# Folding two sections of w_mod on chip, keeping the softmax only transposed, and issuing zero fills from ScalarE in a fused forward and backward block

## The chip, the cores and the metric

One core of one Trainium2 chip runs one program, a single launch with all inputs and outputs in HBM. The metric is device time in microseconds of one execution; beside it stands one execution with the hardware profiler on. The engines are TensorE (PE), VectorE (DVE), ScalarE (ACT), GpSimd (POOL) and SyncE (SP). PE, DVE and ACT compute; in this kernel POOL does nothing but issue transfers after its first microseconds, and SP nothing else at all. 16 DMA engines move the data, whichever engine issued the transfer.

## The reference

One token (D = 1024) goes through an adaLN block: attention over a window of 4096 cached keys (32 query heads, 4 KV heads), then a gated FFN with F = 3584. The outputs are the block's output and the gradients of all its eleven inputs, all bf16.

```python
mod = (silu(c) @ w_mod).reshape(1, 6, 1, -1)          # w_mod [1024, 6144]
sa, ca, ga, sb, cb, gb = (mod[:, i] for i in range(6))
h = layernorm(x) * (1 + ca) + sa
q = h @ wq;  p = softmax(q k^T * Dh**-0.5);  o = p v   # last 4096 of 65536 rows of the caches
x = x + ga * (o @ wo)
h = layernorm(x) * (1 + cb) + sb
x = x + gb * ((sigmoid(h @ w_gate) * (h @ w_up)) @ w_down)
out, vjp = jax.vjp(f, x, k_cache, v_cache, wq, wo, w_gate, w_up, w_down, c, w_mod)
return (out, *vjp(grad_out))
```

The gradients of the two caches have the caches' own shape, [4, 65536, 128]. Of these, 61440 rows of each head lie outside the window and are zero: the kernel writes them as 120 zero fills of 1 MiB each. The gradient of a weight is an outer product of a column and a row, as large as the weight. The gradient that reaches c needs w_mod times the gradient of mod.

## The kernel before

All big data lies in one SBUF tile, `arena`, cut into regions by hand: A (64 KiB of each partition), B and C (32 each), F (40), E (8). The order of every engine is the order of the code (a manual schedule), and each engine issues its transfers in that order.

**Front.** SP loads w_mod (8 tiles of 1.5 MiB, L233), wq (8 of 1 MiB, L237), K and V (L282), wo (L298) and the first w_down blocks. PE multiplies each tile as it lands: `mod_ps` (L257), `q_ps` (L287), transposes of K and V (L318), scores, softmax into a tile of its own, `P_bf`, [128 rows, 4096], its transpose `pT` (L352 to L365), `o_col` (L371), then the product with wo (L417).

**FFN, 7 blocks of 512 columns, L445 to L503.** A block has 1 MiB each of w_down, w_up, w_gate (`wd`, `wu`, `wg`), in five slots of 8 KiB in region F; slot number is `3n`, `3n+1`, `3n+2` modulo 5. So `wg` of block n+1 takes the slot of `wd` of block n once that has been stored, `wd` of n+2 that of `wu` of n, and `wu` of n+2 that of `wg` of n. In a block: PE `gu` (L451), ACT two sigmoids (L455, L456), DVE `dhh` (L458 to L470), PE broadcasts and ACT casts to `du_b`, `dg_b` (L483), DVE overwrites `wd` with its gradient (L485) and POOL stores it (L486); then DVE reduces each of the 8 tiles of `wu` and ACT overwrites it with its gradient (L491, L492), POOL stores it (L493), and the same for `wg` (L498 to L500). POOL also loads `wg` and `wu`; SP loads `wd`. Weights are overwritten in place by their gradients, so a store must land before the next load into that slot.

**Back.** Broadcast of the gradients (L518, L551), wo's part in 8 pieces (DVE L560, ACT L561, store L562; a landed store lets SP load a tile of wq again into that place, L565, tiles 1 to 7, as tile 0 has stayed in region E), the gradient of the scores `dS` (L587, which reads `P_bf`), `dq`, then a loop over 8 tiles (L634 to L644): wq's gradient (L635, L636, stored L637), K's and V's gradients (`grad_kv`, L615 to L629, PE and ACT, stored L628) and, every second turn, a section `sec` (L540): columns 2048 to 6143 of a row tile of w_mod, loaded again by SP (L538), reduced and overwritten by DVE, stored by POOL (L543). At the end, columns 0 to 2047 of w_mod, loaded again by SP as 8 tiles of 512 KiB (L547), are reduced by DVE (L666), and ACT makes their gradient (L667), stored by POOL (L668).

**Zero fills** (`zero`, L124) are put between this work by counts. Before: 42 from POOL in the front, paced by PE, DVE and the counts `Z_MOD` to `Z_LN`; 42 from SP in the FFN, two at each of three places of a block, each with a dependence on the block's work (`Z_FFN`, L489, L494, L503); 36 from POOL in the back.

The transfers of SP and ACT together go round eight completion flags (DMAHW0 to DMAHW7 in the program), those of POOL round another eight (DMASW0 to DMASW7): a transfer waits for the landing of the one that had its flag before it.

Of the kernel before, what the change touches and what calls it, by code (L numbers as in the profile page):

```python
# [10 lines left out]
P = 128  # L11
FP32 = mybir.dt.float32
# [24 lines left out]

Z_MOD, Z_Q, Z_KV, Z_SM, Z_O, Z_WO, Z_LN = 1, 1, 1, 2, 2, 1, 2
Z_FFN = (2, 2, 2)
Z_T0 = 3  # L40
Z_DWO = [1, 1, 1, 1, 1, 1, 1, 6]
Z_SEC = [1, 1, 1, 1, 1, 1, 1, 1]
Z_DWQ = [1, 1, 1, 1, 1, 1, 1, 1]
Z_DKV = [0, 0, 1, 0, 1, 0, 1, 0]


@with_exitstack
def kernel(
# [34 lines left out]

    arena = pool.tile([P, 176 * KIB], BF16, name="arena")

# [3 lines left out]

    A_OFF, B_OFF, C_OFF, F_OFF, E_OFF = 0, 64, 96, 128, 168  # L90

# [77 lines left out]
    def col_to_row_out(col_f, dram_out_row, name):  # L169
        rp = ptp.tile([8, P], FP32, name="rp_" + name, tag="tp")  # L170
        nc.tensor.transpose(rp[:, :], col_f, ident_f[:, :])
        rowb = vt([8, P], name + "_orow", BF16)
        cp(rowb, rp[:, :])
        nc.sync.dma_start(out=dram_out_row.rearrange("o (j p) -> (o j) p", p=P), in_=rowb)
# [60 lines left out]
    wq_t = [ar(E_OFF, 8)] + [ar(A_OFF + 8 * (j - 1), 8) for j in range(1, KD)]  # L235
    for j in range(KD):
        nc.sync.dma_start(out=wq_t[j], in_=wq_view[:, j, :])  # L237

    zero(4)

# [11 lines left out]
    ln1, rstd1 = layernorm_col(x0_col, "ln1")  # L252

    mod_ps = new_acc("mod_ps")
    for j in range(KD):
        for k in range(KM):
            mm = nc.tensor.matmul(mod_ps[:, k:k + 1], lhsT=wm_t[j][:, k * P:(k + 1) * P],  # L257
                                  rhs=cs_bf[:, j:j + 1], start=(j == 0 and k == 0), stop=(j == KD - 1),
                                  skip_group_check=True)
        zero(Z_MOD, mm)  # L260
    mod_col = vt([P, KM], "mod_col")
# [23 lines left out]
    for j in range(KD):  # L285
        for h in range(HQ):
            mm = nc.tensor.matmul(q_ps[:, h:h + 1], lhsT=wq_t[j][:, h * P:(h + 1) * P],  # L287
                                  rhs=h1_bf[:, j:j + 1], start=(j == 0 and h == 0), stop=(j == KD - 1),
                                  skip_group_check=True)
        zero(Z_Q, mm)  # L290
    q_col2 = vt([P, 2 * HQ], "q_col2", BF16)
# [19 lines left out]

    def transpose_kv(src, engs):
        for i in range(16):
            tb, g = divmod(i, G)
            tp = new_tp("tp_kv")
            for t8 in range(8):
                t_ = tb * 8 + t8
                nc.tensor.transpose(tp[:, t8 * P:(t8 + 1) * P], src[:, g, t_ * DH:(t_ + 1) * DH], ident_bf[:, :])  # L318
            o = x_T[:, g, tb * 1024:(tb + 1) * 1024]
            if engs[i] == "A":  # L320
                last = nc.scalar.copy(out=o, in_=tp[:, :])  # L321
            else:
                last = cp(o, tp[:, :])
            if i % 4 == 3:
                zero(Z_KV, last)

    transpose_kv(k_nat, "AV" * 8)
    Q_hd = make_hd(q_col2, "Q_hd")

    P_bf = vt([P, W], "P_bf", BF16)  # L330
    mx8 = vt([P, 8], "mx8")
# [13 lines left out]
    nc.scalar.activation(out=P_bf, in_=P_bf, func=ACT.Exp, bias=nbias[:, 0:1], scale=SCALE, accum_out=ssum)  # L345
    transpose_kv(v_nat, "VVVVVV" + "AV" * 5)
# [3 lines left out]
    zero(Z_SM, last)  # L350

    def transpose_rows(src, name, engs="AVAV"):  # L352
        dst = pool.tile([P, KT, G, HG], BF16, name=name, tag="pTdsT")
        for tb in range(4):
            tp = new_tp("tp_" + name)
            for t8 in range(8):
                t_ = tb * 8 + t8
                nc.tensor.transpose(tp[:, t8 * P:(t8 + 1) * P], src[:, t_ * P:(t_ + 1) * P], ident_bf[:, :])
# [56 lines left out]
    for h in range(HQ):  # L415
        for k in range(KD):
            mm = nc.tensor.matmul(attn_ps[:, k:k + 1], lhsT=wo_t[h // 4][:, h % 4, k * P:(k + 1) * P],  # L417
                                  rhs=o_bf[:, h:h + 1], start=(h == 0 and k == 0), stop=(h == HQ - 1),
                                  skip_group_check=True)
        if h % 4 == 3:  # L420
            zero(Z_WO, mm)
    zero(Z_LN, mm)
# [22 lines left out]
    for n in range(NB):  # L445
# [110 lines left out]
    for q4 in range(8):  # L556
# [24 lines left out]
    for ch in range(8):  # L581
        ps = new_ps("dp_ps")
        for g in range(G):
# [49 lines left out]
    dwq_view = out_4.rearrange("(j p) n -> p j n", p=P)  # L633
    for j in range(KD):  # L634
# [3 lines left out]
        zero(Z_DWQ[j])  # L638
        grad_kv(gkv[8 * j:8 * j + 8], Z_DKV[j])
        if j % 2 == 1:  # L640
            sec(2 + j // 2, Z_SEC[2 + j // 2])
            if j == 1:
                s2_load(6)
                s2_load(7)  # L644

# [66 lines left out]
```

## Time and profile before

| what | value |
|---|---|
| median of 3 runs | 674.62 us (672.17 to 674.93) |
| the profiled execution | 675.23 us |
| its span, first to last instruction | 673.5 us |
| bytes moved in the span | 265.74 MB |
| busy share of the span | DVE 46%, ACT 31%, PE 22%, POOL 14% |

The profiled execution's own time is 1.7 us longer than its span, and 0.6 us longer than the median. A page of the profile gives each engine's busy time, the busy share and rate of the DMA engines in 40 slices of the span, the chain of waits that ended last, groups of equal instructions with what they waited for, and the issues of transfers with the time from issue to landing. `DMA share` in a table of windows is the mean busy share of the 16 DMA engines; 1.0 is all of them.

### The profile page before, as it was taken

To read this page: it belongs to the slowest core of one execution; us is meant where nothing else is said; L and a number is where in the kernel's file an instruction comes from. 1 tells how busy PE (TensorE), PEld (TensorE's weight loads), DVE (VectorE), ACT (ScalarE), POOL (GpSimd) and SP (SyncE) were. 2 spreads that over 40 slices of the span, in tenths; PEclk is the share of its full clock that TensorE was granted. 3 is DMA by queue.
4 is the path that set the end of the run, shared out by engine and by line. 5 is a ranking of instruction groups with operands and counts; after the bars stand their busy time and mean duration, and the time that the engine had idled before them with its cause. 6 is when DMAs were issued, how large, how long until landed. Compare 5 with 4: busy or idle time off the path is not lost.

```text
span 673.5 us, 6855 instructions
## 1 busy us (share of the span) xinstructions
PE 147.2 (22%) x2648; PEld 124.6 (19%) x2648; DVE 307.2 (46%) x604; ACT 209.0 (31%) x304; POOL 96.2 (14%) x161
## 2 busy tenths in 40 slices
PE   2212214661114111111110101304720002333100
PEld 2212213561113101111110001202620001223100
DVE  2000002630008491819180907899842999100790
ACT  1000002730006270707070705796520002334181
POOL 2000100022010101010101010221111111121120
PEclk9999999985555555555555555555755555555555
DMA  8999999999998999999999998999999999999996
GB/s 338 426 428 425 427 425 427 419 419 408 394 423 369 345 377 381 378 373 375 371 380 350 349 415 324 366 422 399 412 416 410 424 425 426 421 423 417 415 407 254
DMA packets 44815, 265.74 MB, mean 395 GB/s; under 512 B 4208, under 2 KB 4208, under 8 KB 19568
## 3 DMA queue, kind: packets, MB, share of 16 engines
q0 software_dynamic: 26640, 156.25, 57.2%
q1 hardware_dynamic: 18096, 109.06, 40.8%
q8 instruction: 20, 0.33, 0.2%
q14 instruction: 11, 0.09, 0.0%
q10 hardware_dynamic: 48, 0.01, 0.0%
HBM read 79.70 MB, written 185.60 MB: 394 GB/s over the span
## 4 chain that ended last, share of the span: by engine, by line
DMA 44%; DVE 8%; issue 5%; ACT 3%; PE 2%; POOL 0%; POOLq 0%; ACTq 0%; DVEq 0%
DMA out_dram<-arena 28%; DMA out_dram<-zeros 9%; DMA arena<-in_B_w_gate_dram 7%; DVE arena L160 4%; DVE junk L160 2%; ACT arena L164 2%; DVE arena L156 1%; PE gu_ps L451 1%; ACT arena L626 1%; ACT arena L624 0%; DVE dug L143 0%; PE ps_kv L620 0%; PE bc_ps L217 0%; ACT dg_b L483 0%; POOL out_dram L500 0%
## 5 line engine op out<-in xcount | busy, mean ns | idle before, releaser
L160 DVE CUSTOM_DVE_ANT_0 arena<-arena 128x4096 bf16<-128x4096 bf16 (+1 forms) x24 | 88.4, 3707 | 22.0 <-DMA arena<-in_w_mod_dram 22.0
L128 POOL DMA_DIRECT2D out_dram<-zeros x78 | 42.4, 544 | 239.8 <-PE mod_ps L257 44.9
L451 PE MATMUL gu_ps<-h_bf,arena 128*128 128x1 bf16 x448 | 16.7, 172 | 156.8 <-DMA arena<-in_B_w_gate_dram 90.4
L321 ACT COPY arena<-tp_kv 128x1024 bf16<-128x1024 bf16 x13 | 13.1, 1010 | 106.2 <-PE tp_kv L318 106.2
L451 PEld LDWEIGHTS <-arena 128*128 128x128 bf16 x448 | 16.1, 118 | 158.5 <-issue 158.5
L143 DVE TENSOR_TENSOR hh<-sg,gu_ps 128x4 f32<-128x4 f32 x7 | 1.1, 159 | 92.4 <-ACT om L456 92.4
L624 ACT CAST arena<-ps_kv 128x512 bf16<-128x512 f32 x32 | 16.1, 697 | 76.1 <-DMA out_dram<-arena 76.1
L160 DVE CUSTOM_DVE_ANT_0 arena<-arena,b1k 128x1024 bf16<-128x1024 bf16 x32 | 36.7, 1218 | 0.0
L160 DVE CUSTOM_DVE_ANT_0 arena<-arena,du_b 128x512 bf16<-128x512 bf16 x56 | 34.9, 689 | 2.0 <-ACT du_b L483 2.0
L164 ACT ACTIVATE arena<-dg_b,h 128x512 bf16<-128x512 bf16 x56 | 35.0, 712 | 0.0
L164 ACT ACTIVATE arena<-du_b,h 128x512 bf16<-128x512 bf16 x56 | 34.9, 712 | 0.0
L160 DVE CUSTOM_DVE_ANT_0 arena<-arena,dg_b 128x512 bf16<-128x512 bf16 x56 | 34.8, 688 | 0.0
L160 DVE CUSTOM_DVE_ANT_0 junk<-arena,b1k 128x1024 bf16<-128x1024 bf16 x28 | 34.2, 1222 | 0.5
L164 ACT ACTIVATE arena<-b1k,o_col 128x1024 bf16<-128x1024 bf16 x32 | 33.4, 1173 | 0.0
L455 ACT ACTIVATE sg<-gu_ps 128x4 f32<-128x4 f32 x7 | 1.2, 173 | 101.1 <-PE gu_ps L451 101.1
L620 PE MATMUL ps_kv<-DO_hd,P_bf 8*128 8x128 bf16 x128 | 15.2, 278 | 76.8 <-ACT arena L624 76.1
L152 DVE COPY arena<-tp_kv 128x1024 bf16<-128x1024 bf16 x19 | 13.0, 691 | 30.3 <-PE tp_kv L318 30.2
L620 PEld LDWEIGHTS <-P_bf 8*128 8x128 bf16 x128 | 11.8, 122 | 80.1 <-issue 78.8
L318 PE MATMUL tp_kv<-ident_bf,arena 128*128 128x128 bf16 x256 | 21.3, 246 | 23.7 <-DMA arena<-in_A_k_cache_dram 15.4
L626 ACT ACTIVATE arena<-ps_kv 128x512 bf16<-128x512 f32 x32 | 16.1, 628 | 31.5 <-DMA out_dram<-arena 31.5
L318 PEld LDWEIGHTS <-arena 128*128 128x128 bf16 x256 | 18.4, 111 | 26.5 <-DMA arena<-in_A_k_cache_dram 16.3
L620 PE MATMUL ps_kv<-Q_hd,arena 8*128 8x128 bf16 x128 | 16.1, 296 | 31.5 <-ACT arena L626 31.5
(179 smaller groups left out, 364.9 us busy)
## 6 DMA issues: line engine op xcount, KB each, us to landing
out_dram<-zeros POOLq DMA_DIRECT2D x78, 1024.0 KB, 23.2
out_dram<-arena POOLq DMA_DIRECT2D x53, 1024.0 KB, 18.5
out_dram<-zeros SPq DMA_DIRECT2D x42, 1024.0 KB, 10.4
arena<-in_A_wq_dram SPq DMA_DIRECT2D x15, 1024.0 KB, 25.5
arena<-in_w_mod_dram SPq DMA_DIRECT2D x8, 1536.0 KB, 27.1
arena<-in_A_wo_dram SPq DMA_DIRECT2D x8, 1024.0 KB, 40.1
arena<-in_w_mod_dram SPq DMA_DIRECT2D x8, 1024.0 KB, 18.2
arena<-in_B_w_up_dram POOLq DMA_DIRECT2D x7, 1024.0 KB, 13.8
```

Of the source, the lines that this page charges most:

```text
L128: ins = (q or nc.gpsimd).dma_start(out=zleft.pop(0), in_=zeros[:, :])
L152: return nc.vector.tensor_copy(out=out, in_=a)
L156: return nc.vector.tensor_scalar(out=out, in0=a, scalar1=s1, scalar2=None, op0=op0)
L160: return nc.vector.tensor_tensor_reduce(out=out, in0=w, in1=b, scale=1.0, scalar=0.0, op0=ALU.mult, op1=ALU.add, accum_out=acc)
L164: return nc.scalar.activation(out=out, in_=b, func=ACT.Copy, scale=col)
L318: nc.tensor.transpose(tp[:, t8 * P:(t8 + 1) * P], src[:, g, t_ * DH:(t_ + 1) * DH], ident_bf[:, :])
L321: last = nc.scalar.copy(out=o, in_=tp[:, :])
L451: nc.tensor.matmul(gu[:, half * 4 + jj:half * 4 + jj + 1], lhsT=w[:, j, jj::4], rhs=h2_bf[:, j:j + 1], start=(j == 0), stop=(j == KD - 1))
L455: nc.scalar.activation(out=sg, in_=gu[:, 0:4], func=ACT.Sigmoid)
L620: nc.tensor.matmul(ps[:, t4 * DH:(t4 + 1) * DH], lhsT=rows[32 * g:32 * g + HG, t_ * P:(t_ + 1) * P], rhs=hd[32 * g:32 * g + HG, :], start= ...
L624: nc.scalar.copy(out=o, in_=ps[:, :])
L626: nc.scalar.activation(out=o, in_=ps[:, :], func=ACT.Copy, scale=float(scale))
```

## The change

1. **w_mod's first two sections.** The gradient to c needs, of columns 0 to 2047, `dsa` times w0 plus `dca` times w1, and `dca` is `dsa` times `ln1`. So w0 + ln1·w1 is formed on chip while w_mod lies there for the forward product (`make_w01`, 2 DVE operations on [128, 1024] for each row tile), and kept in a new region G of 16 KiB. The 8 loads of 512 KiB (L547) are gone, the last DVE reduction is over 1024 columns and not 2048, and the gradient tiles are made by ACT and DVE in turn.
2. **Softmax.** `P_bf` now lies in region F until it has been transposed; `pT` stays. In the back 128 PE transposes and 4 ACT copies rebuild `P_bf` from `pT`, ahead of wo's part.
3. **FFN.** ACT issues the zero fills, at five places of a block and without dependences of their own; SP stores `wd`'s gradient, which POOL did; SP's next load of `wd` stands last in the block.
4. **wq** tile 0 is no longer kept in E: all 8 tiles are loaded again, tile 0 last, and the loop of the back takes them in the order 1 to 7, 0. The loads of `sec` tiles 1 to 6 come after them, that of tile 7 in the loop.
5. **Counts of zero fills**: 29 in the front, 59 in the FFN, 32 in the back, by lists.

```diff
-Z_FFN = (2, 2, 2)
+Z_FFN = [0, 2, 0, 3, 5, 2, 0, 0, 2, 6, 1, 1, 0, 1, 5, 0, 0, 3, 1, 4, 2, 2, 2, 2, 0, 0, 3, 7, 1, 0, 0, 0, 0, 4, 0]
-Z_T0 = 3
+Z_T0 = 6
...
+    w01 = ar(G_OFF, 16).rearrange("p (j n) -> p j n", j=KD)
+    w01_tmp = ar(F_OFF + 32, 4).bitcast(FP32)
+    def make_w01(j):
+        mulv(w01_tmp, wm_t[j][:, D:2 * D], b1k)
+        addv(w01[:, j, :], w01_tmp, wm_t[j][:, 0:D])
...
-    P_bf = vt([P, W], "P_bf", BF16)
+    P_bf = ar(F_OFF + 32, 8)
...
+        zero(Z_FFN[5 * n], None, nc.scalar)
         for jj in range(4):
             last = outer_dve(wd[:, jj, :], hh[:, jj:jj + 1], b1k)
-        nc.gpsimd.dma_start(out=wd_dram(out_8, n), in_=wd_t[n])
+        nc.sync.dma_start(out=wd_dram(out_8, n), in_=wd_t[n])
         if n + 1 < NB:
             load_wg(n + 1)
-        zero(Z_FFN[0], last, nc.sync)
         for j in range(KD):
             ttr(wu[:, j, :], wu[:, j, :], du_b, dh2acc[:, n * 16 + j:n * 16 + j + 1])
             last = outer_act(wu[:, j, :], h2[:, j:j + 1], du_b)
+            if j % 4 == 3:
+                zero(Z_FFN[5 * n + 1 + j // 4], None, nc.scalar)
         nc.gpsimd.dma_start(out=dwu_view[:, :, n * FB:(n + 1) * FB], in_=wu)
...
+    for tb in range(4):
+        tp = new_tp("tp_P")
+        for t8 in range(8):
+            for g in range(G):
+                k = (tb * 8 + t8) * HQ + HG * g
+                nc.tensor.transpose(tp[32 * g:32 * g + 32, t8 * P:(t8 + 1) * P], pT[:, k:k + 32], ident_bf[:, :],
+                                    tile_position=(0, 32 * g))
+        nc.scalar.copy(out=P_bf[:, tb * 1024:(tb + 1) * 1024], in_=tp[:, :])
...
-        ttr(s2_t[j], s2_t[j], dmod_b2, dcs[:, KD + j:KD + j + 1])
-        outer_act(s2_t[j], cs_col[:, j:j + 1], dmod_b2)
+        ttr(w01[:, j, :], w01[:, j, :], dmod_b2[:, 0:D], dcs[:, KD + j:KD + j + 1])
+        if j % 2 == 0:
+            outer_act(s2_t[j], cs_col[:, j:j + 1], dmod_b2)
+        else:
+            outer_dve(s2_t[j], cs_col[:, j:j + 1], dmod_b2)
```

On SP's queue, in the first two blocks of the FFN, stands before (with the flags that each row waits for):

```order
L400 DMA arena<-in_B_w_down_dram 128x4096 [waits DMASW7_49,DMAHW1_49,DMASW0_49,PE_49]
L128 DMA out_dram<-zeros 128x4096 [waits DMAHW2_49,Activation_49]
L128 DMA out_dram<-zeros 128x4096 [waits DMAHW3_49]
L128 DMA out_dram<-zeros 128x4096 [waits DMAHW4_49,DVE_49]
L128 DMA out_dram<-zeros 128x4096 [waits DMAHW5_49]
L128 DMA out_dram<-zeros 128x4096 [waits DMAHW6_49,Activation_49]
L128 DMA out_dram<-zeros 128x4096 [waits DMAHW7_49]
```

and now, at the same place:

```order
L512 DMA out_dram<-arena 128x4096 [waits DMAHW5_49,DMAHW3_49,DVE_49]
L426 DMA arena<-in_B_w_down_dram 128x4096 [waits DMASW1_49,DMASW7_49,PE_49,Activation_49]
L512 DMA out_dram<-arena 128x4096 [waits DMAHW4_49,DMAHW2_49,DVE_49]
L426 DMA arena<-in_B_w_down_dram 128x4096 [waits DMASW5_49,DMAHW5_49,PE_49,Activation_49]
L512 DMA out_dram<-arena 128x4096 [waits DMAHW6_49,DMAHW3_49,DVE_49]
```

The zero fills with their waits for DVE and ACT have left SP; in their place stands the store of `wd`'s gradient, which waits for DVE.

On ScalarE, from the end of the first block to the second block's first gradient tiles, stands before:

```order
L164 ACTIVATE arena<-dg_b,h_1712 128x512 x8
L455 ACTIVATE sg_1976<-gu_ps 128x4
L456 ACTIVATE om_1977<-gu_ps 128x4
L483 CAST du_b<-bc_ps 128x4x128
L483 CAST dg_b<-bc_ps 128x4x128
L164 ACTIVATE arena<-du_b,h_1712 128x512 x8
```

and now:

```order
L172 ACTIVATE arena<-dg_b,h_1730 128x512 [waits DVE_49] x4
L136 DMA out_dram<-zeros 128x4096 [waits DMAHW4_49]
L136 DMA out_dram<-zeros 128x4096 [waits DMAHW5_49]
L136 DMA out_dram<-zeros 128x4096 [waits DMAHW6_49]
L136 DMA out_dram<-zeros 128x4096 [waits DMAHW7_49]
L136 DMA out_dram<-zeros 128x4096 [waits DMAHW0_49]
L480 ACTIVATE sg_1997<-gu_ps 128x4 [waits PE_49]
L481 ACTIVATE om_1998<-gu_ps 128x4
L508 CAST du_b<-bc_ps 128x4x128 [waits PE_49,Activation_49]
L508 CAST dg_b<-bc_ps 128x4x128 [waits PE_49,Activation_49]
L136 DMA out_dram<-zeros 128x4096 [waits DMAHW1_49]
L136 DMA out_dram<-zeros 128x4096 [waits DMAHW3_49]
```

Five zero fills now stand on ScalarE ahead of the next block's sigmoid, and two behind its casts, each with a wait for a flag of an earlier transfer.

On ScalarE at the start of the back stands before:

```order
L222 CAST b1k<-bc_ps 128x512
L222 CAST arena<-bc_ps 128x512 x8
L164 ACTIVATE arena<-b1k,o_col 128x1024 x32
L362 COPY dsT<-tp_dsT 128x256 x4
L222 CAST arena<-bc_ps 128x512 x8
```

and now:

```order
L230 CAST b1k<-bc_ps 128x512
L230 CAST arena<-bc_ps 128x512 x8
L584 COPY arena<-tp_P 128x1024 x4
L172 ACTIVATE arena<-b1k,o_col 128x1024 x32
L389 COPY pT<-tp_dsT 128x256 x4
L230 CAST arena<-bc_ps 128x512 x8
```

The four copies of the rebuilt softmax stand ahead of the 32 operations that make wo's gradient.

More of the change, by code (lines that the diff above doesn't have):

```diff
@@ L35 @@
 KIB = 512
-Z_MOD, Z_Q, Z_KV, Z_SM, Z_O, Z_WO, Z_LN = 1, 1, 1, 2, 2, 1, 2
-Z_FFN = (2, 2, 2)
-Z_T0 = 3
[L41 to L44, printed above, removed]
+Z_INIT = 5
+Z_MOD = [0, 1, 0, 1, 0, 0, 0, 0]
+Z_Q = [2, 0, 0, 1, 0, 1, 0, 2]
+Z_K = [0, 1, 0, 1]
+Z_V = [0, 3, 0, 0]
+Z_SM = 4
+Z_O = 1
+Z_WO = [0, 0, 1, 1, 4, 0, 0, 0]
+Z_LN = 0
+Z_FFN = [0, 2, 0, 3, 5, 2, 0, 0, 2, 6, 1, 1, 0, 1, 5, 0, 0, 3, 1, 4, 2, 2, 2, 2, 0, 0, 3, 7, 1, 0, 0, 0, 0, 4, 0]
+Z_T0 = 6
+Z_DWO = [1, 0, 1, 1, 1, 2, 0, 5]
+Z_SEC = [1, 2, 0, 0, 0, 2, 2, 7]
+Z_DWQ = [0, 2, 0, 2, 0, 0, 2, 3]
+Z_DKV = [0, 1, 1, 0, 0, 1, 1, 0]
 @with_exitstack
@@ L82 @@
     ptp = ctx.enter_context(tc.tile_pool(name="ptp", bufs=2, space=bass.MemoryType.PSUM))
-    arena = pool.tile([P, 176 * KIB], BF16, name="arena")
+    arena = pool.tile([P, 184 * KIB], BF16, name="arena")
     def ar(off, size):
         return arena[:, int(off * KIB):int((off + size) * KIB)]
-    A_OFF, B_OFF, C_OFF, F_OFF, E_OFF = 0, 64, 96, 128, 168
+    A_OFF, B_OFF, C_OFF, F_OFF, G_OFF = 0, 64, 96, 128, 168
     def vt(shape, name, dt=FP32):
@@ L171, in col_to_row_out @@
         nc.tensor.transpose(rp[:, :], col_f, ident_f[:, :])
-        rowb = vt([8, P], name + "_orow", BF16)
+        rowb = pool.tile([8, P], BF16, name=name + "_orow", tag="orow")
         cp(rowb, rp[:, :])
@@ L234 @@
         wm_t.append(t)
-    wq_t = [ar(E_OFF, 8)] + [ar(A_OFF + 8 * (j - 1), 8) for j in range(1, KD)]
+    wq_t = [ar(A_OFF + 8 * ((j + 7) % 8), 8) for j in range(KD)]
     for j in range(KD):
         nc.sync.dma_start(out=wq_t[j], in_=wq_view[:, j, :])
-    zero(4)
+    zero(Z_INIT)
     tp0 = ptp.tile([P, 24], BF16, name="tp_rows", tag="tp")
@@ L252 @@
     ln1, rstd1 = layernorm_col(x0_col, "ln1")
+    ln1_bf = vt([P, KD], "ln1_bf", BF16)
+    cp(ln1_bf, ln1)
+    b1k = vt([P, D], "b1k", BF16)
+    bcast(ln1_bf, KD, b1k, "A")
+    w01 = ar(G_OFF, 16).rearrange("p (j n) -> p j n", j=KD)
[3 more added lines that the diff above has]
+        addv(w01[:, j, :], w01_tmp, wm_t[j][:, 0:D])
     mod_ps = new_acc("mod_ps")
@@ L259 @@
                                   skip_group_check=True)
-        zero(Z_MOD, mm)
+        if j < KD - 1:
+            make_w01(j)
+        zero(Z_MOD[j], mm)
     mod_col = vt([P, KM], "mod_col")
@@ L289 @@
                                   skip_group_check=True)
-        zero(Z_Q, mm)
+        zero(Z_Q[j], mm)
     q_col2 = vt([P, 2 * HQ], "q_col2", BF16)
@@ L324, in transpose_kv @@
             if i % 4 == 3:
-                zero(Z_KV, last)
-    transpose_kv(k_nat, "AV" * 8)
+                zero(nz[i // 4], last)
+    transpose_kv(k_nat, "AV" * 8, Z_K)
     Q_hd = make_hd(q_col2, "Q_hd")
-    P_bf = vt([P, W], "P_bf", BF16)
+    P_bf = ar(F_OFF + 32, 8)
     mx8 = vt([P, 8], "mx8")
@@ L350 @@
     zero(Z_SM, last)
+    pT = vt([P, KT * HQ + 32], "pT", BF16)
+    nc.vector.memset(pT[:, KT * HQ:], 0.0)
     def transpose_rows(src, name, engs="AVAV"):
-        dst = pool.tile([P, KT, G, HG], BF16, name=name, tag="pTdsT")
+        dst = pT[:, 0:KT * HQ].rearrange("p (t g h) -> p t g h", t=KT, g=G)
         for tb in range(4):
@@ L420 @@
         if h % 4 == 3:
-            zero(Z_WO, mm)
+            zero(Z_WO[h // 4], mm)
     zero(Z_LN, mm)
@@ L499 @@
             last = outer_act(wg[:, j, :], h2[:, j:j + 1], dg_b)
+            if j % 4 == 3:
+                zero(Z_FFN[5 * n + 3 + j // 4], None, nc.scalar)
         nc.gpsimd.dma_start(out=dwg_view[:, :, n * FB:(n + 1) * FB], in_=wg)
@@ L502 @@
             load_wu(n + 2)
-        zero(Z_FFN[2], last, nc.sync)
+        if n + 2 < NB:
+            load_wd(n + 2)
     ffn = vt([P, KD], "ffn")
@@ L531 @@
     dcs = vt([P, 2 * KD], "dcs")
-    sec_off = [F_OFF + 24, F_OFF + 32, A_OFF + 56, C_OFF + 16, C_OFF + 24, B_OFF, B_OFF + 8, B_OFF + 16]
+    sec_off = [F_OFF + 32, C_OFF + 16, C_OFF + 24, B_OFF, B_OFF + 8, B_OFF + 16, B_OFF + 24, F_OFF + 24]
     sec_t = [ar(o, 8) for o in sec_off]
-    s2_off = [B_OFF + 24, B_OFF + 28, F_OFF + 24, F_OFF + 28, F_OFF + 32, F_OFF + 36, A_OFF + 56, A_OFF + 60]
-    s2_t = [ar(o, 4) for o in s2_off]
+    s2_t = [ar(A_OFF + 4 * j, 4) for j in range(KD)]
+    P_bf = ar(F_OFF + 24, 8)
     def sec_load(j):
@@ L563 @@
         zero(Z_DWO[q4])
-        if q4 < 7:
-            nc.sync.dma_start(out=wq_t[q4 + 1], in_=wq_view[:, q4 + 1, :])
-    sec_load(2)
+        j = (q4 + 1) % 8
+        nc.sync.dma_start(out=wq_t[j], in_=wq_view[:, j, :])
     do_col2 = vt([P, 2 * HQ], "do_col2", BF16)
@@ L594 @@
     dq_ps, mm = av_like(k_nat, dsT, "dq")
-    sec_load(5)
-    sec_load(6)
-    sec_load(7)
+    for k in range(3, 7):
+        sec_load(k)
     dq_bf = vt([P, HQ], "dq_bf", BF16)
@@ L633 @@
     dwq_view = out_4.rearrange("(j p) n -> p j n", p=P)
-    for j in range(KD):
+    for i in range(KD):
+        j = (i + 1) % 8
         ttr(wq_t[j], wq_t[j], dq_b, dh1[:, j:j + 1])
@@ L637 @@
         nc.gpsimd.dma_start(out=dwq_view[:, j, :], in_=wq_t[j])
[L638 to L644, printed above, removed]
+        zero(Z_DWQ[i])
+        grad_kv(gkv[8 * i:8 * i + 8], Z_DKV[i])
+        if i == 4:
+            sec_load(7)
+        if i % 2 == 1:
+            sec(2 + i // 2, Z_SEC[2 + i // 2])
     dln1 = vt([P, KD], "dln1")
```

21 lines of the change are left out of this document (6 added, 15 removed).

## Prediction

> **What bounds the kernel now.** I read the page first, then a table of windows by stage.
>
> ```profile
> span 673.5 us, 6855 instructions
> ...
> DMA  8999999999998999999999998999999999999996
> GB/s 338 426 428 425 427 425 427 419 419 408 394 423 369 345 377 381 378 373 375 371 380 350 349 415 324 366 422 399 412 416 410 424 425 426 421 423 417 415 407 254
> DMA packets 44815, 265.74 MB, mean 395 GB/s; under 512 B 4208, under 2 KB 4208, under 8 KB 19568
> ```
>
> ```profile
> 10.00:205.00 195.00, 60.71 (x1382) 53.71 (x1383) 25.92 (x67) 26.34 (x32) 23.59 (x41) 0.84 1.02 420
> 205.00:424.00 219.00, 30.58 (x715) 27.71 (x712) 122.21 (x357) 86.65 (x141) 25.81 (x32) 0.50 0.95 368
> 424.00:640.00 216.00, 54.79 (x552) 42.53 (x552) 138.12 (x152) 77.20 (x121) 37.96 (x67) 0.52 1.01 414
> 640.00:660.00 20.00, 0.38 (x1) 0.08 (x1) 18.10 (x23) 16.01 (x8) 4.94 (x11) 0.50 1.01 405
> 660.00:673.50 13.50, 0.00 (x0) 0.00 (x0) 0.00 (x0) 0.00 (x0) 0.49 (x1) 0.50 0.54 217
> ```
>
> The last two columns are the DMA share and GB/s. The DMA engines bound the kernel: in the front (10 to 205 us) and the back (424 to 660) they are all busy, at 405 to 420 GB/s, while no compute engine is busy for more than two thirds of a long stage. The FFN (205 to 424) is the exception: 368 GB/s at a share of 0.95. I went on into one of its blocks by windows, then by the chain of waits (start, length, what).
>
> ```profile
> 265.40:272.70 7.30, 3.23 (x72) 2.83 (x72) 5.42 (x15) 1.71 (x4) 0.89 (x2) 0.50 0.90 281
> 272.70:290.10 17.40, 1.20 (x32) 1.14 (x32) 12.13 (x36) 10.60 (x17) 0.56 (x1) 0.50 1.00 417
> 290.10:299.40 9.30, 0.05 (x2) 0.08 (x3) 0.00 (x0) 0.00 (x0) 2.65 (x3) 0.50 1.00 381
> 272.70:299.40 26.70, 1.24 (x34) 1.22 (x35) 12.13 (x36) 10.60 (x17) 3.21 (x4) 0.50 1.00 404
> ```
>
> ```profile
> 272.69 16.89 DMA out_dram<-arena
> ...
> 290.15 9.07 DMA arena<-in_B_w_gate_dram
> ...
> 306.60 16.46 DMA out_dram<-arena
> ```
>
> A block takes 33.9 us (272.69 to 306.60), and 26.0 of them are two transfers one behind the other: the store of w_down's gradient, then the load of w_gate into the freed slot. While SP's zero fills flow, the rate is 417. When they have run out and only w_gate's load and two gradient stores are left it is 381, and during the block's compute 281. The zero fills come in bursts tied to the block's work, and so leave these holes.
>
> **The change, part by part.** First the bytes, by the issues of transfers (count, size, median us to landing):
>
> ```profile
> out_dram<-zeros POOLq DMA_DIRECT2D x78, 1024.0 KB, 23.2
> out_dram<-zeros SPq DMA_DIRECT2D x42, 1024.0 KB, 10.4
> arena<-in_A_wq_dram SPq DMA_DIRECT2D x15, 1024.0 KB, 25.5
> arena<-in_B_w_up_dram POOLq DMA_DIRECT2D x7, 1024.0 KB, 13.8
> arena<-in_B_w_gate_dram POOLq DMA_DIRECT2D x7, 1024.0 KB, 9.6
> arena<-in_B_w_down_dram SPq DMA_DIRECT2D x7, 1024.0 KB, 6.6
> arena<-in_w_mod_dram SPq DMA_DIRECT2D x8, 512.0 KB, 12.1
> ```
>
> The eight 512 KB loads of w_mod go (4.19 MB) and one load of wq comes (1.05 MB): 3.15 MB less. The 120 zero fills stay, but 13 leave the front, 17 come into the FFN and 4 leave the back.
>
> *Front.* 13 fills of 1.05 MB are 13.6 MB, at 420 GB/s 32.5 us less, if the DMA engines stay busy. What could become late is the compute between the landing of K and the product with wo:
>
> ```profile
> 111.23 2.83 PE L318 MATMUL tp_kv<-ident_bf,arena 128*128 128x128 bf16 x24 [3.86 <-DMA arena<-in_A_k_cache_dram]
> ...
> 150.37 0.72 PE L417 MATMUL attn_ps<-o_bf,arena 128*128 128x1 bf16 x22 [0.50 <-DVE o_bf L152]
> ```
>
> That is 39.1 us, in which 16.4 MB can move. V's loads (4.2), wo's (8.4) and 5 to 9 fills (5.2 to 9.4) by the new counts make 17.8 to 22.0 MB: enough, by little. Then the FFN's first loads are free. The new DVE work is 16 operations on [128, 1024], which no row shows; the bounds are the 128x1024 rows below, 536 ns with one input and twice 1218 with two inputs (a float result is twice as wide): 9 to 39 us. I take 20, by the two-input row. It lies where DVE waited 42.0 us for the last product with w_mod; only the last tile's pair comes behind that wait, and it stands after `h1_bf`, so PE's product with wq is not held. Cost: nothing, and at the upper end still nothing.
>
> ```profile
> DVE mod_col L152 <- PE mod_ps L257: 42.0, 1, 42.0
> DVE arena L160 <- DMA arena<-in_w_mod_dram: 22.0, 1, 22.0
> POOL out_dram L128 <- DMA out_dram<-arena: 40.1, 16, 4.5
> POOL out_dram L128 <- DMA out_dram<-zeros: 29.9, 12, 4.5
> POOL arena L406 <- DMA out_dram<-arena: 68.4, 4, 18.3
> ```
>
> ```profile
> L160 DVE CUSTOM_DVE_ANT_0 arena<-arena,b1k 128x1024 bf16<-128x1024 bf16 x32 | 36.7, 1218 | 0.0
> L164 ACT ACTIVATE arena<-b1k,o_col 128x1024 bf16<-128x1024 bf16 x32 | 33.4, 1173 | 0.0
> L160 DVE CUSTOM_DVE_ANT_0 arena<-arena 128x2048 bf16<-128x2048 bf16 x8 | 17.8, 2286 | 0.0
> L156 DVE TENSOR_SCALAR arena<-b1k,hh 128x1024 bf16<-128x1024 bf16 x28 | 13.3, 536 | 0.0
> L321 ACT COPY arena<-tp_kv 128x1024 bf16<-128x1024 bf16 x13 | 13.1, 1010 | 106.2 <-PE tp_kv L318 106.2
> L358 PE MATMUL tp_dsT<-ident_bf,arena 128*128 128x128 bf16 x32 | 3.6, 313 | 0.0
> ```
>
> *FFN, the chain of a block.* w_down's gradient no longer stands behind w_up's load in POOL's queue, but alone on SP's, where the load of w_down, the nearest row, landed in 6.6 us: 16.9 becomes 6.6. The load of w_gate now runs beside fills, as w_up's did (13.8): 9.1 becomes 13.8. The chain is then 33.9 − 16.9 + 6.6 − 9.1 + 13.8 = 28.3 us. But a block's transfers are 6 MiB of weights and gradients and on average 59/7 = 8.4 fills, 15.1 MB, which at 404 GB/s need 37.4 us. So the transfers bound the block, with 9.1 us to spare, and the holes close. The stage moved 219.0 us × 368 = 80.6 MB; with 17 fills (17.8 MB) it is 98.4. At 404, the row of a stretch in which something was always queued, strided transfers included, it takes 243.6 us, 24.6 more than now. The ends are 417 (236.0 us) and 381 (258.3).
>
> *FFN, ScalarE's queue.* The new wait: each fill waits there for the landing of the transfer that had its flag before it, eight issues back on SP and ACT together. Behind it wait the next sigmoid, so DVE and PE, and the gradients of `wu` and `wg`, so POOL's stores and the loads into their slots. The issue itself is short (min/median/max ns):
>
> ```profile
> L128 SPq DMA_DIRECT2D out_dram<-zeros x42: 332/422/1344, 212.1 to 423.6; - x42
> ```
>
> 59 × 0.42 = 25 us over the stage, 3.5 per block (11.3 at the maximum). ACT is busy 86.65 of 219 us and can take it. A wait for a flag means that up to eight transfers are under way, 1.05 MB each, 20 us of DMA time at 420; the chain from sigmoid to the next store is about 8 us (299.4 to 306.60 in the block above). So the engines should not run dry by such a wait. I price it at nothing; where it isn't, see the second rival.
>
> Against this part speaks a rule of the Trainium skill (page "DMA: Bandwidth & Descriptors", section "Issuing engines are not separate DMA queues"): transfers of all issuers end on the same 16 DMA engines, and issuing from several saves only the sequencer's issue time. By it the stage would keep its 368 GB/s, and the sum would be 673. The trace agrees that the engines are shared; but 417 and 281 in one block show that what is queued sets the rate.
>
> *Back.* 4 fills and 3.15 MB of loads less are 7.34 MB, at 414 GB/s 17.7 us. Rebuilding the softmax: 128 transposes at 3.6/32 = 0.113 us are 14.4 us on PE, and the last of four copies 1.0: ACT starts its 32 products 15.4 us later, behind them the stores of wo's gradient and the loads of wq. It is covered by three more fills (`Z_T0`) and by the queue: POOL's fills land 23.2 us after issue, and DVE has 22.0 us of waiting for w_mod's loads further on. The cover could fail in part: 0 to 15.4, I take 2, by the 22.0. The tail's DVE work falls from 8 × 2.29 to 8 × 1.22 + 4 × 2 × 0.54 = 14.1, 4.2 us, with the engines' share still 1.01 until 660: nothing, at most 4 us gained.
>
> *Sum.* 673.5 − 32.5 + 24.6 − 17.7 + 2 = 649.9 us of span. The profiled execution took 1.7 us more than its span, and the median lies 0.6 below it: **651 us**.
>
> **The rivals.** *First: the split over queues brings no rate.* The FFN stays at 368: 98.4 MB take 267.4 us, and 649.9 + 23.8 + 1.1 = 674.8, without the 2 us for the rebuild 672.8: **673 us**. This is what the rule above would make of it; for it speaks that the rate of strided transfers alone is 381, against it the 417. *Second: ScalarE is held by its fills.* The place is the 20 fills that the list puts last in the first four blocks (5, 6, 5, 4), right ahead of the next sigmoid. It decides from 9.1 us of holding per block. If each waits 4.5 us, the longest wait of POOL's fills for a landing, the holds are 22.5, 27, 22.5 and 18, and 90 − 4 × 9.1 = 53.6 us are added: **705 us**, slower. For it: POOL's fills waited 70.0 us so in 28 waits. Against: they did so while the engines were full. *Third: the rebuild is not covered,* and the engines run dry ahead of wo's stores: 13.4 us more, **664 us**. For it: 32 ACT products are a fixed 33.4 us behind it. Against: the 22.0 us of slack.
>
> **How the numbers follow.** The forecast has 0.70, the first rival 0.11, the second 0.07, the third 0.12. Its own ends are 417 without the rebuild's cost (651 − 7.6 − 2 = 641, a little less with the tail) and 381 (665.7); the third rival lies inside, so 640 to 668 leaves out the first and second, 0.18. A measurement of this kernel can tell 0.5% from no change, 3.4 us: faster means below 671.2. Faster: 0.70 + 0.12 and a quarter of the first rival, 0.85; the rest of that, 0.08, is the same; slower 0.07.
>
> **What would show it.** The bytes should read 262.6 MB. A window over the FFN should show about 98 MB at 400 GB/s or more and a share near 1.0; 370 means the first rival. Waits of w_gate's load for w_down's store should fall from 68.4 us, and that store should land in 6 to 8. ACT's waits for transfers between a block's last product and the next sigmoid, beside a low DMA share, would show the second. A share under 0.95 in the 30 us after the FFN would show the third. The front should end near 172 us; a hole there between K's landing and wo's product would make the first term wrong.

## The result, and the profile after

The changed kernel took 653.05 us (median of 4 runs, 651.23 to 654.42), the kernel before 673.39 us (median of 4, 669.6 to 674.93) on the same chip: a ratio of 0.970, 95% interval 0.965 to 0.976. The profiled execution took 652.61 us with a span of 650.8 us, where before had 675.23 and 673.5. These are the span, the DMA engines' busy tenths, their rate in 40 slices, and the bytes.

```profile
span 650.8 us, 7106 instructions
...
DMA  8999999999999999999999999999999999999996
GB/s 335 430 428 422 426 426 413 404 418 397 421 425 415 416 417 393 414 388 408 417 356 419 361 409 415 392 382 412 388 415 422 415 425 426 425 407 388 410 411 251
DMA packets 43810, 262.63 MB, mean 404 GB/s; under 512 B 4096, under 2 KB 4096, under 8 KB 18432
```

Before, the slices of the FFN (13th to 26th) read 324 to 381, but for one of 415. Now (11th to 26th) they are mostly 388 to 425, with two of 356 and 361, and a row of 9s runs through the busy tenths. The span splits in two: 262.63 MB at the old mean (265.74 MB in 673.5 us, 394.6 GB/s) would take 665.6 us, so the bytes are worth 7.9 us; the other 14.8 us are the higher rate.

By stage, in the changed kernel (start:end, length, busy time of PE, PEld, DVE, ACT and POOL, granted clock, DMA share, GB/s):

```profile
10.00:160.60 150.60, 61.77 (x1370) 55.16 (x1371) 45.01 (x85) 26.75 (x34) 14.91 (x26) 0.90 1.02 419
160.60:419.00 258.40, 32.50 (x739) 29.29 (x739) 123.56 (x366) 89.27 (x142) 21.83 (x25) 0.50 1.01 404
419.00:620.00 201.00, 54.31 (x672) 42.31 (x672) 128.64 (x138) 88.16 (x129) 37.12 (x63) 0.54 1.01 409
620.00:640.00 20.00, 0.37 (x1) 0.08 (x1) 19.36 (x31) 0.00 (x0) 5.29 (x10) 0.50 1.01 406
640.00:650.80 10.80, 0.00 (x0) 0.00 (x0) 0.25 (x1) 0.00 (x0) 0.00 (x0) 0.50 0.46 180
```

The FFN (160.60 to 419.00) now runs at a share of 1.01 and 404 GB/s, the stages around it as before. The waits (who, for what, total us, times, longest) have moved with it:

```profile
POOL arena L429 <- DMA out_dram<-arena: 134.4, 5, 30.2
POOL arena L432 <- DMA out_dram<-arena: 28.0, 4, 8.5
```

```profile
ACT sg L480 <- PE gu_ps L476: 76.3, 7, 14.7
ACT arena L172 <- DMA arena<-in_B_w_down_dram: 32.3, 3, 11.1
ACT arena L172 <- issue: 15.6, 5, 12.3
```

POOL waits less for w_down's store ahead of w_gate's load (28.0 us for 68.4) and more ahead of w_up's (134.4 for 60.8). The two together are longer than before (162.4 us for 129.2), so these waits do not say that a block's chain became shorter. ScalarE is in fact held: three of its waits end with the landing of a w_down load, an SP transfer, as a fill ahead takes over that load's flag. One block in the chain of waits:

```profile
243.61 16.43 DMA out_dram<-arena
...
261.52 14.67 DMA arena<-in_B_w_gate_dram
...
284.25 16.80 DMA out_dram<-arena
```

A block takes 40.6 us here. Store, w_gate's load and compute follow one another as before. The store is as long as before (16.43 us for 16.89) and w_gate's load longer (14.67 for 9.07), but the DMA engines no longer idle meanwhile.

### The profile page after: what moved, and what is told of

It is laid out like the page before. It is cut to its first block, busy times and chain, and to the rows that moved or that the text cites. A ratio compares the mean times of both kernels' runs of the same rounds, so it can differ in the third digit from the quotient of the medians.

```text
span 650.8 us, 7106 instructions
## 1 busy us (share of the span) xinstructions
PE 149.7 (23%) x2784; PEld 127.4 (20%) x2784; DVE 319.7 (49%) x626; ACT 206.9 (32%) x306; POOL 83.0 (13%) x137
## 2 busy tenths in 40 slices
DMA packets 43810, 262.63 MB, mean 404 GB/s; under 512 B 4096, under 2 KB 4096, under 8 KB 18432
## 4 chain that ended last, share of the span: by engine, by line
DMA 64%; DVE 14%; ACT 11%; PE 6%; issue 4%; POOL 0%; SPq 0%; POOLq 0%; ACTq 0%; DVEq 0%
DMA out_dram<-arena 28%; DMA arena<-in_B_w_gate_dram 18%; DMA arena<-in_w_mod_dram 7%; DVE arena L168 6%; DMA arena<-in_A_wq_dram 6%; ACT arena L172 5%; DMA arena<-in_A_k_cache_dram 5%; DVE junk L168 3%; PE tp_kv L342 2%; DVE arena L164 1%; ACT arena L345 1%; PE gu_ps L476 1%; ACT arena L230 1%; ACT du_b L508 1%; DMA out_dram<-dx_orow 1%
## 5 line engine op out<-in xcount | busy, mean ns | idle before, releaser
L168 DVE CUSTOM_DVE_ANT_0 arena<-arena 128x4096 bf16<-128x4096 bf16 (+1 forms) x24 | 80.1, 3350 | 51.4 <-DMA arena<-in_w_mod_dram 51.4
L136 POOL DMA_DIRECT2D out_dram<-zeros x61 | 33.6, 554 | 185.0 <-PE q_ps L311 49.8
L172 ACT ACTIVATE arena<-du_b,h 128x512 bf16<-128x512 bf16 x56 | 35.3, 710 | 36.0 <-DMA arena<-in_B_w_down_dram 32.3
L649 PEld LDWEIGHTS <-arena 8*128 8x128 bf16 x256 | 24.9, 127 | 106.1 <-issue 102.7
L172 ACT ACTIVATE arena<-dg_b,h 128x512 bf16<-128x512 bf16 x56 | 35.3, 708 | 26.4 <-issue 14.4
L653 ACT CAST arena<-ps_kv 128x512 bf16<-128x512 f32 x32 | 16.1, 691 | 77.2 <-DMA out_dram<-arena 77.2
L172 ACT ACTIVATE arena<-b1k,o_col 128x1024 bf16<-128x1024 bf16 x32 | 33.4, 1142 | 0.0
L649 PE MATMUL ps_kv<-DO_hd,arena 8*128 8x128 bf16 x128 | 15.3, 280 | 77.9 <-ACT arena L653 77.2
L429 POOL DMA_DIRECT2D arena<-in_B_w_up_dram x7 | 6.2, 890 | 134.4 <-DMA out_dram<-arena 134.4
L655 ACT ACTIVATE arena<-ps_kv 128x512 bf16<-128x512 f32 x32 | 16.1, 624 | 21.8 <-DMA out_dram<-arena 21.8
```

What stands on the lines that cost most here:

```text
L136: ins = (q or nc.gpsimd).dma_start(out=zleft.pop(0), in_=zeros[:, :])
L168: return nc.vector.tensor_tensor_reduce(out=out, in0=w, in1=b, scale=1.0, scalar=0.0, op0=ALU.mult, op1=ALU.add, accum_out=acc)
L172: return nc.scalar.activation(out=out, in_=b, func=ACT.Copy, scale=col)
L649: nc.tensor.matmul(ps[:, t4 * DH:(t4 + 1) * DH], lhsT=rows[32 * g:32 * g + HG, t_ * P:(t_ + 1) * P], rhs=hd[32 * g:32 * g + HG, :], start= ...
L653: nc.scalar.copy(out=o, in_=ps[:, :])
L655: nc.scalar.activation(out=o, in_=ps[:, :], func=ACT.Copy, scale=float(scale))
```

## The experiments

Theory: the kernel is bound by its transfers, so the gain is the 3.15 MB less plus the FFN's holes, which close because enough fills lie beside each block's chain. Rivals: the fold costs what it saves; the new queues (a third issuer, the store by itself on SP) and not the number of fills close the holes. The kernels of each of the three groups below ran on one chip beside the kernel before (675.4 to 675.5 us), and I compare ratios to it.

**First group: the change in halves, and its queues undone.** `e1_fold_only` gives the FFN back its old issue order and all counts of fills, and keeps the fold, the rebuild and the loads of wq.

```diff
-Z_FFN = [0, 2, 0, 3, 5, 2, ...]   # and the lists of 29 and 32 around it
+Z_FFN = (2, 2, 2)                 # 42 in the front, 36 in the back
...
-        zero(Z_FFN[5 * n], None, nc.scalar)
...
-        nc.sync.dma_start(out=wd_dram(out_8, n), in_=wd_t[n])
+        nc.gpsimd.dma_start(out=wd_dram(out_8, n), in_=wd_t[n])
...
+        zero(Z_FFN[0], last, nc.sync)
...
```

> The changed kernel with the FFN as it was: the fills from SP with their dependences, two at each of three places, w_down's gradient stored by POOL, the counts 42 / 42 / 36. Theory (bytes plus holes): only the 3.15 MB are saved, 7.6 us at 414 GB/s, so 666 us, and the FFN keeps its 368 GB/s and its 219 us. Rival (the fold and the rebuild cost what they save, up to 13.4 us of uncovered rebuild): 673 to 679 us. Second rival (the fold is worth more than its bytes, by the shorter tail and fewer loads in the back): 660 us or less.

Measured: 664.56 us, 0.984 (0.980 to 0.989), 10.7 us less (7.6 to 13.7). The forecast 7.6 lie at the edge of the interval. The first rival falls.

`e2_queues_only` is the complement: the kernel before with the changed FFN lines and lists.

> The kernel before with only the FFN's new issue order and the new counts: fills from ScalarE, w_down's gradient stored by SP, its next load last in the block, 29 / 59 / 32 fills; no fold, no rebuild. Theory: the FFN's holes close, so the time is that of the changed kernel plus 7.6 us for the 3.15 MB, 660 us, with the FFN at 400 GB/s or more. Rival (the gain is in the fold): 670 us or more.

Measured: 661.37 us, 0.980 (0.975 to 0.984), and its FFN runs at 404 GB/s from 160.6 to 419. The two halves give 10.7 + 13.8 = 24.5 us, the whole 20.0 to 21.2 (0.970 and, measured again in the third group, 0.969), so they add up within their intervals.

`e3_store_pool` changes one word of the changed kernel:

```diff
-        nc.sync.dma_start(out=wd_dram(out_8, n), in_=wd_t[n])
+        nc.gpsimd.dma_start(out=wd_dram(out_8, n), in_=wd_t[n])
```

> The changed kernel with one thing undone: POOL stores w_down's gradient. Theory (what counts is that fills are always queued, not the length of a block's chain): 653 us, within 3 us, though the load of w_gate waits longer for the store. Rival (the store on its own queue shortened the chain): the store stands behind w_up's load again, a block's chain grows by up to 10 us over 37.4 us of transfers, and the time rises to 665 us or more.

Measured: 658.10 us, 0.974 (0.971 to 0.978). That is between the two: 2.7 to 3.9 us above the changed kernel (by its ratio of 0.970 and by that of the third group, 0.969), with intervals that overlap. The 665 of the rival did not come, but a small gain from the move may be there.

`e4_fills_sp` takes the fills from ScalarE (`last_c` is the second broadcast's copy, `last` the product ahead):

```diff
-        zero(Z_FFN[5 * n], None, nc.scalar)
+        zero(Z_FFN[5 * n], last_c, nc.sync)
-                zero(Z_FFN[5 * n + 1 + j // 4], None, nc.scalar)
+                zero(Z_FFN[5 * n + 1 + j // 4], last, nc.sync)
```

> The changed kernel with the same 59 fills at the same places of a block, but issued by SP, each with a dependence on the ScalarE instruction ahead of it. Theory (the number of fills under way counts, not who issues them): they start at the same moments, ScalarE is no longer held (32 us of waits at L172 go), 650 to 655 us. Rival (a third queue is what raises the rate): the fills stand in one queue with the store and the load of w_down, the FFN falls towards 368 to 381 GB/s and the time to 663 us or more.

Measured: 655.18 us, 0.970 (0.966 to 0.973), the changed kernel's ratio. In its trace ScalarE's gradient products (L172) no longer wait for a transfer at all. So ScalarE's holds and ScalarE as issuer together change nothing that can be told; a small cost and a small gain that cancel are not excluded.

**Second group: number against queue.** `e5_42_fills` is the changed kernel with the old number of fills in the FFN; `e6_old_59` is `e1` with nearly the new number.

```diff
-Z_FFN = [0, 2, 0, 3, 5, 2, ...]
+Z_FFN = [1, 1, 1, 1, 2] * 7      # e5: 42 fills, new queues; front 42, back 36
...
-Z_FFN = (2, 2, 2)
+Z_FFN = (3, 3, 2)                # e6: 56 fills, old queues; front 29, back 35
```

> The changed kernel with 42 fills in the FFN instead of 59 (one at each of the five places of a block, two at the last), still from ScalarE; 42 in the front and 36 in the back, as before. Theory (the number of fills in the FFN is what closes its holes): a block has 6.3 MB of weights and gradients and 6.3 MB of fills, 31 us at 404 GB/s, less than its chain, so the engines run dry; about the time of the run with only the fold, 0.984 of the time before, 662 to 665 us. Rival (their own queue, issued without dependences, closes the holes): 0.970, 653 to 655 us.

> The fold with the FFN's old issue order (fills from SP with dependences at three places, w_down's gradient stored by POOL, its next load in the middle of the block), but 3, 3 and 2 fills at these places, 56 in all, 29 in the front and 35 in the back. Theory (the number counts): 0.970 to 0.975 of the time before, 654 to 658 us. Rival (the queues count, the number doesn't): 0.984, 662 to 665 us.

Measured: `e5` 662.69 us, 0.981 (0.977 to 0.985); `e6` 657.31 us, 0.973 (0.970 to 0.977). With the old queues, going from 42 to 56 fills is worth 0.011 (`e1` to `e6`, intervals apart). With 42 fills, the new queues are worth 0.004 (`e1` to `e5`, intervals overlap). The number decides the greater part. The stretch from 210 to 390 us lies inside the FFN in all kernels; its row for before, `e1`, `e5`, `e6` and the changed kernel, and then for `e3` and `e4`, in this order:

```profile
210.00:390.00 180.00, 24.19 (x560) 21.93 (x560) 101.80 (x293) 73.64 (x118) 21.52 (x26) 0.50 0.96 367
```

```profile
210.00:390.00 180.00, 24.19 (x560) 21.94 (x560) 101.47 (x293) 73.52 (x118) 22.23 (x27) 0.50 0.97 376
```

```profile
210.00:390.00 180.00, 24.17 (x560) 21.93 (x560) 100.15 (x292) 73.53 (x118) 20.41 (x23) 0.50 0.98 385
```

```profile
210.00:390.00 180.00, 20.09 (x480) 18.28 (x481) 82.44 (x237) 60.70 (x100) 19.90 (x24) 0.50 1.01 403
```

```profile
210.00:390.00 180.00, 18.91 (x448) 17.12 (x448) 75.49 (x218) 60.27 (x96) 16.87 (x20) 0.50 1.00 400
```

```profile
210.00:390.00 180.00, 18.91 (x449) 17.10 (x448) 82.02 (x238) 57.96 (x92) 19.77 (x24) 0.50 0.99 386
```

```profile
210.00:390.00 180.00, 18.91 (x448) 17.11 (x448) 74.63 (x216) 53.20 (x87) 17.70 (x20) 0.50 0.99 390
```

The last two columns (share, GB/s) go up with the fills: 0.96 to 0.98 and 367 to 385 with 42, 0.99 to 1.01 and 386 to 403 with 56 or 59. Within each number the queues still shift the rate (376 to 385 from `e1` to `e5`; 386 and 390 in `e3` and `e4` for 400 in the changed kernel), and one stretch of one trace is too little to price that; in the times it is at most 0.006 of the ratio (`e3`, 0.974 for 0.969). From before to the changed kernel, PE's busy time goes the other way (24.19 to 18.91 us, with 560 products and 448): the blocks follow more slowly, and that is right, because each block carries more bytes.

`e7_even_list` spreads the 59 fills evenly over the places:

```diff
-Z_FFN = [0, 2, 0, 3, 5, 2, ...]
+Z_FFN = [2, 2, 2, 1, 2] * 3 + [2, 1, 2, 1, 2] * 4
```

> The changed kernel with its 59 fills of the FFN spread evenly (2, 2, 2, 1, 2 in three blocks, 2, 1, 2, 1, 2 in four) in place of the list. Theory (the total counts): within 3 us of the changed kernel, 0.970. Rival (where in a block they stand counts; evenly spread, fewer are held back for the time when a block's own transfers have run out): 0.975 or more, 657 us and up.

Measured: 655.81 us, 0.971 (0.967 to 0.975). The list's order brings nothing that can be told.

`e8_no_rebuild` leaves out the loop `for tb in range(4)` of the rebuild, so the gradients of the scores read other values.

> The changed kernel without the rebuild of the softmax: its 128 transposes and four copies are left out, so the gradients of the scores read other values. It prices the rebuild. Theory (the fills and transfers under way cover it): 0 to 2 us less than the changed kernel. Rival (it stands on the path ahead of wo's stores): 6 us less by the copies' time in the changed kernel's trace, up to 13 us by the price in the prediction.

Measured: 651.67 us, 0.965 (0.962 to 0.969), 4 us under `e7` and 2.3 us (0.969 to 0.965) under the changed kernel of the third group. Both pairs of intervals overlap, so this alone settles nothing.

**Third group: the rebuild's place, and the point where fills stop helping.** `e9_changed_again` is the changed kernel as the measure of this group; `e10_rebuild_later` moves the rebuild into wo's loop.

```diff
...
         nc.gpsimd.dma_start(out=dwo_view[:, q4 * 4:(q4 + 1) * 4, :], in_=wo_t[q4])
+        if q4 % 2 == 1:
+            rebuild(q4 // 2)        # 32 transposes, one copy
```

> The changed kernel itself, beside the next three on one chip, as their measure. Expected: 0.970 of the time before, as measured first.

> The changed kernel with the rebuild of the softmax not ahead of wo's part but inside it, one quarter behind each second piece, where nothing waits for it yet; a candidate for a faster version. The run without the rebuild took 0.965, 3.5 us less than the changed kernel's 0.970. If that was the rebuild standing ahead of wo's stores, 3 to 4 us less than the changed kernel run beside this one. If the transfers cover the rebuild (the DMA share reads 1.0 there), no difference beyond 2 us.

Measured: 653.59 us, 0.969 (0.966 to 0.971), and 653.48 us, 0.969 (0.966 to 0.972). ScalarE starts wo's products 7 us earlier in `e10`, and the time is the same: the transfers cover the rebuild's place. What leaving it out altogether is worth stays open between 0 and 4 us.

`e11_50_fills` and `e12_70_fills` vary the number, with what they take or give in the back.

```diff
+Z_FFN = [2, 2, 1, 1, 2] + [1, 2, 1, 1, 2] * 6   # e11: 50; back 41
...
+Z_FFN = [2] * 35                                # e12: 70; back 21
```

> The changed kernel with 50 fills in the FFN (2, 2, 1, 1, 2 in the first block, 1, 2, 1, 1, 2 in the others) and 41 in the back, the front's 29 kept. Theory (fills bring time only until a block's transfers last as long as its chain, 31 to 33.5 us with 42 fills): 7.1 fills and 6.3 MB are 13.8 MB, 34.1 us at 404 GB/s, just over the chain, so no loss: within 2 us of the changed kernel. Rival (each fill in the FFN brings its share, in proportion, from 42 to 59): 9 of 17 fills' worth lost, half of the 0.010 by which 42 fills are slower, 3.4 us more.

> The changed kernel with 70 fills in the FFN, two at each of its 35 places, and 21 in the back. Theory: the FFN was already bound by its transfers with 59, so nothing more is gained: within 2 us, or up to 4 us more if the back now runs dry. Rival (in proportion): 11 of 17 fills' worth gained, 4.4 us less.

Measured: `e11` 658.36 us, 0.975 (0.972 to 0.978); `e12` 655.28 us, 0.971 (0.968 to 0.974). With 70 nothing more is gained, as the theory had it: its FFN goes to 406 GB/s (210 to 390 us), and its back (430 to 600 us) falls from the changed kernel's 413 to 401. But 50 fills are not enough, and there my theory missed; the rival's 3.4 us came (4.8). The windows of five of `e11`'s blocks, from store to store, show why:

```profile
205.00:245.00 40.00, 4.37 (x104) 3.99 (x104) 17.11 (x50) 12.35 (x21) 3.54 (x4) 0.50 0.96 383
245.00:280.50 35.50, 4.48 (x105) 3.99 (x104) 17.88 (x53) 13.58 (x22) 3.54 (x4) 0.50 0.97 387
280.50:317.00 36.50, 4.43 (x104) 4.00 (x104) 16.75 (x50) 11.56 (x20) 3.75 (x5) 0.50 0.99 387
317.00:350.00 33.00, 4.42 (x104) 3.99 (x104) 17.52 (x51) 12.83 (x21) 3.45 (x4) 0.50 1.00 397
350.00:388.00 38.00, 4.43 (x104) 4.00 (x104) 16.83 (x50) 12.03 (x21) 3.54 (x4) 0.50 0.91 360
```

They take 33.0 to 40.0 us, 36.6 on average, not the 34.1 of their bytes. I had taken the chain from the run with 42 fills (31 to 33.5 us). The chain is no fixed length, though: a block takes 31 to 33.5 us with 42 fills, 36.6 with 50 and 38.8 with 59 (the changed kernel, from 164.5 to 397.1 us). That the fills stretch it because they share the DMA engines with it is my reading; no run shows it apart. At 50 the chain still outlasts the block's transfers, so holes stay (shares of 0.96, 0.97 and 0.91).

## Why the prediction was right, and where it was not

**The total** came out at 653 for 651. **The bytes** are as counted, 262.63 MB, and `e1` prices the fold at 7.6 to 13.7 us.

**The front** ended at 160.6 us, not near 172, and the FFN moved 258.4 us × 404 = 104.4 MB, not 98.4. These are one miss: by the difference, some 5 to 6 MB that the front moved before now lie behind the first `gu`. The first load of w_gate is one of them, as it lands at 164.5 us; the others I did not trace. The sum doesn't see it, and the FFN's end, forecast at 673.5 − 249.5 − 32.5 + 24.6 = 416.1, was 419. No hole opened between K and wo's product, the share of the front was 1.02. The new DVE work, priced at 20 us from rows that do something else, is now a row of its own:

```profile
L151 DVE TENSOR_TENSOR arena<-arena 128x1024 bf16<-128x1024 f32 x8 | 9.8, 1225 | 0.3
L151 DVE TENSOR_TENSOR arena<-arena,b1k 128x1024 f32<-128x1024 bf16 x8 | 9.8, 1224 | 18.4 <-DMA arena<-in_w_mod_dram 16.5 <-ACT b1k L230 1.8
```

19.6 us, in idle time of DVE, and the share there stays at 1.02. Right.

**The FFN's rate** was right: 404 in the window, share 1.01; the first rival (368) falls. **The FFN's chain was the step that failed.** It said that w_down's store, alone on SP's queue, lands in 6.6 us, the chain shrinks to 28.3 us, and the transfers have 9.1 us to spare. The store's time to landing (min/median/max) before, on POOL's queue, then in the changed kernel, then in `e5` with 42 fills and the changed kernel's queues:

```profile
DMA to landing us min/median/max: 7.5/16.7/18.2
```

```profile
DMA to landing us min/median/max: 10.7/13.8/16.8
```

```profile
DMA to landing us min/median/max: 7.0/10.3/12.2
```

Neither the queue nor the number of fills alone sets it: with 59 fills the median is 14.4 us from POOL (`e3`), 13.8 from SP in the changed kernel and 17.0 from SP with the even list (`e7`). In the changed kernel's chain of waits the six stores that w_gate's load waits for take 10.94 to 16.80 us, so the 6.6 us of the sum are nowhere to be seen. Nor is the store alone on SP's queue. Between one store and the next stands a load of w_down, each time but the last. In the block above that load went out at 283.82 us and the store behind it at 284.25, though the store's data had been ready at 282.98 (timeline of the changed kernel: the products that make w_down's gradient, the load, the store):

```profile
281.30 1.68 DVE L164 TENSOR_SCALAR arena<-b1k,hh 128x1024 bf16<-128x1024 bf16 x4
...
283.82 0.33 SPq L426 DMA_DIRECT2D arena<-in_B_w_down_dram  x1
...
284.25 1.17 SPq L512 DMA_DIRECT2D out_dram<-arena  x1
```

The chain grew to about 39 us a block instead of shrinking to 28.3, and `e11` shows that it already outlasts the transfers at 7.1 fills a block. There were no 9.1 us to spare. The forecast held because the engines stay busy while the chain waits, and by luck in the count: 59 was enough to cover a chain that had been priced 10 us too short, and with 50 holes would have stayed. The prediction had also said that the old fills "come in bursts tied to the block's work, and so leave these holes". `e6` keeps those bursts and their dependences, with only more fills in each, and has the rate of 403: the fills were too few.

Against the change I had weighed the Trainium skill's "DMA: Bandwidth & Descriptors", section "Issuing engines are not separate DMA queues", and made it forecast 673. The runs bear the rule out (`e4`: another issuer, the same time); it was my conclusion from it that was wrong, since the number of fills had changed as well as their issuer.

**ScalarE's queue**, priced at nothing, cost nothing that can be told, though the holds came (32.3 us in three waits, up to 11.1): `e4` has none and is no faster. An issue took longer there than the 0.42 us of the prediction, 0.725 us at the median, and that shows no cost either. The second rival falls, by the reason given: the engines stayed full meanwhile.

**The rebuild**, 15.4 us ahead of wo's products in the prediction, is shorter (timeline of the changed kernel: start, length, what):

```profile
422.71 1.09 PE L582 MATMUL tp_P<-ident_bf,pT 128*32 128x128 bf16 x64
...
423.43 2.94 ACT L584 COPY arena<-tp_P 128x1024 bf16<-128x1024 bf16 x3
...
428.94 1.01 ACT L584 COPY arena<-tp_P 128x1024 bf16<-128x1024 bf16 x1 [2.58 <-PE tp_P L582]
...
429.85 3.22 ACT L172 ACTIVATE arena<-b1k,o_col 128x1024 bf16<-128x1024 bf16 x3
```

ScalarE comes to wo's products 6.4 us after the first copy began (423.43 to 429.85), and `e10` shows that its place ahead of them is covered; the DMA share in the 30 us after the FFN (419 to 449) reads 1.01. The 2 us taken are inside what `e8` leaves open (0 to 4); the third rival's 13.4 are not. **The back** took 650.8 − 419.0 = 231.8 us, forecast 249.5 − 17.7 + 2 = 233.8. So the span's near hit, 650.8 for 649.9, holds two small misses that partly cancel: the FFN's end 2.9 us late, the back 2.0 us short.

## What to carry to other kernels

Where a stage is a chain of dependent transfers, look at the DMA share in that stage alone, and move independent transfers into it from stages that are full anyway, until the share reads 1.0; who issues them mattered little here (0.969 to 0.974 with 59 fills). Don't price the chain as if it kept its length: with what fills the holes the chain grew too, so put in clearly more than the sum of the bytes asks for (here 59 where the sum said 50), and stop where the stage they are taken from begins to run dry (70).

## What the runs showed of the hardware that I had not expected

Transposes of 32 columns, put on four column groups of PE in turn, follow one another much faster than those of 128 columns. To compare them the granted clock must be the same, and it isn't the same everywhere. These are windows over the rebuild's first 64 transposes, in the changed kernel and in `e10` (granted clock, DMA share and GB/s stand last):

```profile
422.50:424.00 1.50, 1.30 (x67) 0.98 (x66) 1.50 (x5) 1.50 (x4) 0.95 (x2) 0.90 0.98 366
```

```profile
421.50:424.00 2.50, 2.09 (x67) 1.73 (x65) 2.50 (x7) 2.50 (x5) 0.80 (x2) 0.51 1.03 387
```

At 0.90 the 64 took 1.09 us, 17 ns each; at 0.51 they took 1.90 us, 30 ns each. The 128-column transposes behind the prediction's 113 ns ran at a clock of 0.50 (469 to 473 us of the kernel before), and the same ones took 67 ns each in the changed kernel at 0.97 (16 in 1.07 us). So at a like clock the narrow ones took about a quarter of the time; whether by the four groups or by the narrower operand, no run separates. The prediction's 14.4 us for 128 of them were far too high, by both the shape and the clock. What remained ahead of wo's products was mostly ScalarE's four copies and a wait of 2.6 us for which the profile shows no cause.

A 1 MiB store on SP's queue landed in 7.0 to 12.2 us beside 42 fills and in 10.7 to 16.8 beside the 59 of the changed kernel. The number of fills is not all of it: with the same 59 spread evenly (`e7`) it took 16.1 to 17.6, with 70 (`e12`) 10.3 to 15.6.
